# Backward pass of sliding-window attention and a gated unit: another unit order, another filler rule, and a few far units turned by DMA

## The chip, the core and the metric

The kernel runs on one core of one Trainium2 chip. The metric is the device time of one execution in microseconds; a value given for a version is the median of its runs. The profile is one further execution, recorded by the hardware profiler; its times are counted from the first instruction of the span. PE is the matrix engine (TensorE), PEld its weight load, ACT is ScalarE, DVE is VectorE, POOL is GpSimd, SP is the engine that only issues transfers.

## The reference

Input x is 2048 rows of 512 bf16 numbers. Branch A is attention with 32 heads of 16 numbers and a causal window of 256 rows; branch B is a gated unit of width 1376. A sigmoid gate g mixes them. The kernel gives the output and the gradients of all seven inputs that carry one.

```python
qkv = (x @ wqkv) -> q, k, v            # 32 heads of 16
scores = q k^T * 16**-0.5              # kept where 0 <= row - col < 256
a = softmax(scores) v @ wo
gate = x @ W_gate ; up = x @ W_up
b = (relu(gate) * up) @ W_down
out = g * a + (1 - g) * b              # g = sigmoid(sum(x * gate_w))
# then the vector-Jacobian product of out with grad_out, for x, wqkv, wo, W_gate, W_up, W_down, gate_w
```

## The kernel before, in words

The kernel has three stages, written one after the other. The first (up to about 252 us) is the gated unit forward and backward. The second is the attention, forward and backward together. The third (from about 718 us) makes the output and the gradient of x. The change is in the second stage only.

**Units.** The attention goes through four head groups c of eight heads each. In a head group it goes through 16 blocks j of 128 query rows. A block meets up to three key blocks kb: its own (role d, the diagonal), the one before (m, the middle) and the one before that (f, the far one), because the window is two blocks wide. The eight heads are taken in two halves of four. A unit is one (c, j, kb, half): 90 in a head group, 360 in all. `units` (L657 to L673) is the list in order. In a block with all three roles the order is m0 f0 d0 m1 d1 f1 (role and half).

**What a unit does.** The main loop (L886) counts steps n, and each engine gets its instructions in the order in which the loop writes them, so this order is the queue of each engine. Unit n makes its scores on PE at step n (`front`, L683, tile ST), ACT takes the exponential (L693, tile Pu), POOL masks it for the roles d and f (L695, L698). At step n+1 PE makes dP (`front_dp`, L707, tile dPT), at n+2 DVE multiplies them (`gradp`, L712, tile Pd). At step n+4 PE makes the row sums and the forward output (`rowsum`, L721 and L723, eight small matmuls into tile BA). Pu and Pd are also needed turned by 128x128 blocks, for the key side (`flip`): either by one DMA from SP for both halves of a pair (L740, written at n+3), or by eight transposes on PE into a PSUM tile `pt` and one copy out of it by ACT or DVE in turn (L750, L752, written at n+4, behind `rowsum`). In head groups 0 to 2 the roles d and m go by DMA, and f by PE.

**The key side.** Five or more steps after a block's last row sums, `cd_piece` (L532) uses the turned tiles, eight small matmuls for each (query block, key block, half), one or two pieces in a step, first in, first out.

**Fillers.** Beside the units PE has work that can be put anywhere: the projections of the next 512 rows (`project_parts`: Q, dO, rows by DMA, K, V, KV; one list `prq` for each quarter of a head group), and the weight gradient of the head group before (`grad_parts`, 16 pieces in `bgq`; four pieces add up in one PSUM tile `wps`, and the fourth copies it out). `credit` decides when: each step earns something, each filler costs something. `held` is true while a weight gradient has been begun and not finished; L957 then goes on with it, and L960 takes a projection only while `held` is false.

**PSUM.** It has eight banks here: four for ST and dPT (tag M), one for the key side (CD), one for BA, and two of tag TR (L523, `attpr`). The tag TR is used by `pt` of `flip`, by `pp` of the projections (L130), by `ptp` of KV (L173) and, for the weight gradients of head groups 0 and 1, by `wps` (L633); these are made during head groups 1 and 2. A PSUM tile is given up when its last reader has read it.

**Buffers in SBUF.** Pair tiles of role m and d have a ring of three each (L688 to L690, tags PPm and PPd); Pu and Pd of role f have two each.

Of the kernel before, what the change touches and what calls it, by code (L numbers as in the profile page):

```python
# [11 lines left out]
BF = mybir.dt.bfloat16  # L12
# [10 lines left out]
def kernel(  # L23
# [20 lines left out]
    nc = tc.nc  # L44
    P = 128
# [10 lines left out]
    DC = D // P  # L56
# [3 lines left out]
    NTG = S // TGW  # L60
# [43 lines left out]
    NP = P // 32  # L104
# [7 lines left out]
    if True:  # L112
        HH = HG // 2
# [4 lines left out]
        def spread(gi, k):  # L118
            rows = slice(32 * k, 32 * k + 32)
            nc.vector.tensor_copy(zt[gi % ZB][rows, :, k, :, :].rearrange("p w t q -> p w (t q)"),  # L120
                                  proj[groups[gi]]["z"][rows, :, :])
# [76 lines left out]
    with ExitStack() as p1, tc.manual_schedule():  # L198
# [43 lines left out]
        half = TPG // 2  # L242
# [105 lines left out]
        for fc in range(FC):  # L348
            for tg in range(NTG):
                k = Step()  # L350
# [97 lines left out]
        for n in range(N1 + 8):  # L448
# [29 lines left out]
            if at(6):  # L478
                f = weights(at(6))
# [34 lines left out]
    if True:  # L514
# [4 lines left out]
        wk = p3b.enter_context(tc.tile_pool(name="attw", bufs=2))  # L519
# [5 lines left out]
        P2 = {}  # L525
# [87 lines left out]
        def load_gw():  # L613
            nc.sync.dma_start(gw_b[:], gate_w.partition_broadcast(P))

        plan = {2: [load_gw], 5: turns("wqkv", A_wqkv, 0, 4, "p0"), 7: turns("wqkv", A_wqkv, 4, 8, "p1"),
                11: turns("wqkv", A_wqkv, 8, 12, "p2"),
                12: turns("Wg", B_W_gate, 0, 4, "x0") + turns("Wg", B_W_gate, 4, 8, "d0"),
                13: turns("Wg", B_W_gate, 8, 12, "x1") + turns("Wu", B_W_up, 0, 4, "d1") + [lambda: clear("Wg")],
                14: turns("Wu", B_W_up, 4, 8, "x2") + turns("Wu", B_W_up, 8, 12, "d2"),  # L620
                15: loads("Wd", B_W_down, 0, "x3") + [lambda: clear("Wu")] + loads("Wd", B_W_down, 4, "d3") + loads("Wd", B_W_down, 8, "p3") + [load_wo]}
# [35 lines left out]
        units = []  # L657
        for c in range(DC):
            for j in range(NT):
                kbs = [k for k in (j - 1, j, j - 2) if k >= 0]  # L660
                for half in range(2):
                    order = kbs if half or len(kbs) < 3 else [kbs[0], kbs[2], kbs[1]]
                    for ki, kb in enumerate(order):
                        u = Unit()
                        u.c, u.j, u.kb, u.half = c, j, kb, half
                        u.first = ki == 0 and half == 0
                        u.last = ki == len(kbs) - 1 and half == 1
                        u.role = ("d", "m", "f")[j - kb]
                        u.pair = u.role == "d" or (u.role == "m" and (c < DC - 1 or j in (3, 5, 7, 9)))
                        u.own = u.role == "f"  # L670
                        u.dma = u.pair or (u.role == "m" and half == 0 and (c < DC - 1 or j < 10))
                        units.append(u)
        NU = len(units)  # L673

        pairs = {}

        def front(u):
            tg, jl = u.j // TPG, u.j % TPG
            z = zt[(u.c * NTG + tg) % ZB]
            KTt = proj[(u.c, u.kb // TPG)][f"K{u.half}"]  # L680
            ksl = slice((u.kb % TPG) * P, (u.kb % TPG + 1) * P)
            ST = ps.tile([P, HH, P], F32, tag="M", bufs=4, name="ST")
            nc.tensor.matmul(ST[:], lhsT=KTt[:, ksl], rhs=z[:, 0, :, jl, :], start=True, stop=True)  # L683
            if not u.own:
                if u.half == 0:
                    kind = "m" if u.c == DC - 1 and u.j == 12 else u.role
                    tag = f"PP{kind}"
                    pairs[(u.c, u.j, u.kb)] = wk.tile([P, 2, 2, HH, P], BF, tag=tag, bufs=3, name=tag)  # L688
                u.PP = pairs[(u.c, u.j, u.kb)][:, u.half, :, :, :]
                u.Pu, u.Pd = u.PP[:, 0, :, :], u.PP[:, 1, :, :]  # L690
            else:
                u.Pu = wk.tile([P, HH, P], BF, tag="Pu", bufs=2, name="Pu")
            nc.scalar.activation(u.Pu[:], ST[:], ACT.Exp)  # L693
            if u.role == "d":
                nc.gpsimd.affine_select(out=u.Pu[:], in_=u.Pu[:], compare_op=ALU.is_ge, fill=0.0, base=0,  # L695
                                        pattern=[[0, HH], [1, P]], channel_multiplier=-1)
            elif u.role == "f":
                nc.gpsimd.affine_select(out=u.Pu[:], in_=u.Pu[:], compare_op=ALU.is_ge, fill=0.0, base=-1,  # L698
                                        pattern=[[0, HH], [-1, P]], channel_multiplier=1)
# [7 lines left out]
            nc.tensor.matmul(u.dPT[:], lhsT=VTt[:, ksl], rhs=z[:, 1, :, jl, :], start=True, stop=True)  # L707

        def gradp(u):
            if u.own:  # L710
                u.Pd = wk.tile([P, HH, P], BF, tag="Pd", bufs=2, name="Pd")
            nc.vector.tensor_tensor(out=u.Pd[:], in0=u.Pu[:], in1=u.dPT[:], op=ALU.mult)  # L712

        def rowsum(u):
# [17 lines left out]
        def flip(u):  # L732
            key = (u.c, u.j, u.kb, "p2")
            if u.role != "f" and key not in P2 and not (u.pair and u.half == 0):
                P2[key] = wk.tile([P, 2, 2, HH, P], BF, tag=f"P2{u.role}", bufs=3, name=f"p2{u.role}")
            if u.dma:
                if u.pair and u.half == 0:
                    return
                hs = slice(0, 2) if u.pair else slice(u.half, u.half + 1)
                nc.sync.dma_start_transpose(out=P2[key][:, hs, :, :, :].rearrange("p b a h q -> p (b a h) q"),  # L740
                                            in_=pairs[(u.c, u.j, u.kb)][:, hs, :, :, :].rearrange("p b a h q -> p (b a h q)"))
                for b in range(2)[hs]:
                    P2[(u.c, u.j, u.kb, b)] = P2[key][:, b, :, :, :]
                return
            eng = ("act", "dve", "act")[copier["i"] % 3] if u.c == 0 else ("act", "dve")[copier["i"] % 2]
            copier["i"] += 1
            pt = psr.tile([P, 2, HH, P], BF, tag="TR", name="pt")
            for a, src in enumerate((u.Pu, u.Pd)):
                for hh in range(HH):
                    nc.tensor.transpose(pt[:, a, hh, :], src[:, hh, :], ident[:])  # L750
            p2 = P2[key][:, u.half, :, :, :] if u.role == "m" else wk.tile([P, 2, HH, P], BF, tag="P2f", bufs=4, name="p2")[:]
            evac(p2, pt[:], eng)  # L752
            P2[(u.c, u.j, u.kb, u.half)] = p2
# [94 lines left out]
        with tc.manual_schedule():  # L848
            ev = {}
            cdq = []  # L850
            bgq = []
            prq = []
# [3 lines left out]
            n = 0  # L856

            held = False
            fed = 1
            early = []  # L860
            late = []

            def background():
                f, more = bgq.pop(0)
                store = f()
                if store is not None:
                    copies.append(store)
                    if len(copies) > 2 or gi + 2 >= len(groups):
                        ev.setdefault(n + 2, []).append(("dma", flush))
                return more  # L870

            def flush():
                while copies:
                    copies.pop(0)()

            def pieces():
                nonlocal credit
# [8 lines left out]
            while n <= NU + LAG or ev or cdq or bgq:  # L886
                now = ev.pop(n, [])
                u = units[n] if n < NU else None
                if u is not None:
                    gi = u.c * NTG + u.j // TPG  # L890
                    if u.first and u.j == 0:
                        sts[u.c] = st.tile([P, NT, 4, P], BF, tag="rows_st", name="rows_st")
                    if u.first and u.j % TPG == 0:
                        if gi + 1 < len(groups):
                            prq = project_parts(*groups[gi + 1]) if gi else second
# [54 lines left out]
                if n >= NU:  # L950
                    if bgq:
                        held = background()
                    elif n > NU + 1:
                        for _ in range(2):
                            if len(S2["grads"]) > DC:
                                S2["grads"].pop(0)()
                elif held and credit > 0.3:  # L957
                    held = background()
                    credit -= 0.65
                elif prq and not held and ((credit > 0.4 and n > fed + 1) or due - n <= len(prq)):  # L960
                    fed = n
                    credit -= (0.44, 0.86, 0.86, 0.1, 0.86, 0.86)[len(prq) - 1]
                    prq.pop(0)()
                    if len(prq) == 4:
                        for k in range(NP):
                            ev.setdefault(n + 1 + k, []).append(("dve", lambda gi=gi, k=k: spread(gi + 1, k)))
                        ev.setdefault(n + 1, []).append(("dma", flush))
                    if not prq:
                        late += plan.get(gi + 1, [])
                elif bgq and len(prq) <= 2 and credit > 0.3:  # L970
                    held = background()
                    credit -= 0.65
# [164 lines left out]
```

## Time and profile before

| | us |
|---|---|
| median of 2 runs | 910.07 |
| the two runs | 909.61 and 910.52 |
| the profiled execution | 911.05 |
| its span in the profile | 909.4 |
| first scores of head groups 0, 1, 2, 3 | 251.7, 353.6, 469.1, 585.0 |
| last scores (unit 359) | 703.0 |

The four head groups thus last 101.9, 115.5, 115.9 and 118.0 us; the first one has no weight gradients beside it. Read the profile as follows. The busy share of an engine is a union of its instructions, and a matmul is recorded with the time until its result is there (a 128x512 matmul 378 ns), while the next one starts before that (0.215 us after it). So the share of PE says how seldom it is empty, and the start-to-start distance says what a matmul costs the queue.

### The profile page before, as it was taken

How to read it: one execution, taken by the hardware profiler on the slowest of the kernel's cores; microseconds unless marked ns; L12 is line 12 of the kernel's file. 1: busy time of each engine (PE TensorE's matmuls, PEld its weight loads, DVE VectorE, ACT ScalarE, POOL GpSimd, SP SyncE). 2: the span in 40 equal slices, each digit the busy share in tenths (PEclk: the TensorE clock that was granted, in tenths of full speed). 3: DMA queues.
4: the chain of work that ended last, by engine and by line, in shares of the span. 5: the costliest groups of instructions: out<-in, count | busy, mean ns of one | idle time of the engine just before them, and what ended most of it. 6: DMA issues, size and time to landing. Idle time of an engine off the chain costs nothing.

```text
span 909.4 us, 26127 instructions
## 1 busy us (share of the span) xinstructions
PE 895.0 (98%) x10711; PEld 566.7 (62%) x10711; DVE 511.8 (56%) x952; ACT 441.3 (49%) x778; POOL 491.7 (54%) x937
## 2 busy tenths in 40 slices
PE   9999999999989999999999999999999999999998
PEld 5555656655657777667776677766777644444445
DVE  4433334324468887678886788876787222333223
ACT  6422232222278777667776677766788211100001
POOL 4644545545267778767777567875677312222221
PEclk9999999999999999999999999999999999999999
DMA  9998879999799999999999989999999998777731
GB/s 301 203 194 186 197 179 207 211 207 216 180 143 158 180 188 194 184 175 156 177 185 187 180 161 182 187 182 184 184 185 186 235 269 227 186 181 185 182 86 46
DMA packets 505575, 169.06 MB, mean 186 GB/s; under 512 B 433456, under 2 KB 504336, under 8 KB 505456
## 3 DMA queue, kind: packets, MB, share of 16 engines
q1 hardware_dynamic: 484816, 145.51, 86.8%
q10 hardware_dynamic: 19008, 17.31, 7.2%
q0 software_dynamic: 1632, 4.59, 1.4%
q8 instruction: 83, 1.36, 0.6%
q14 instruction: 36, 0.29, 0.1%
HBM read 32.28 MB, written 36.24 MB: 75 GB/s over the span
## 4 chain that ended last, share of the span: by engine, by line
PE 80%; DMA 5%; DVE 4%; POOL 3%; issue 3%; SPq 2%; ACT 2%; ACTq 0%; POOLq 0%; DVEq 0%
PE dxps L1062 8%; PE ST L683 8%; PE dPT L707 7%; PE pt L750 6%; PE wps L412 5%; PE wps L637 5%; PE dxps L1066 4%; PE CD L541 4%; PE bps L1035 4%; PE BA L721 4%; PE pp L133 4%; PE dps L414 3%; PE ups L363 3%; PE gps L363 2%; PE CD L544 2%
## 5 line engine op out<-in xcount | busy, mean ns | idle before, releaser
L683 PE MATMUL ST<-z,K 128*128 128x512 bf16 x360 | 135.8, 378 | 2.6 <-DVE PPm L712 1.2
L707 PE MATMUL dPT<-z,V 128*128 128x512 bf16 x360 | 136.0, 378 | 1.9 <-DVE Pd L712 0.5
L695 POOL TENSOR_SCALAR_AFFINE_SELECT PPd<-PPd 128x512 bf16<-128x512 bf16 x126 | 80.0, 635 | 86.7 <-ACT PPd L693 86.7
L377 POOL TENSOR_TENSOR hT<-rg,upm 128x512 bf16<-128x512 bf16 x44 | 51.8, 1176 | 116.0 <-DVE upm L375 104.3
L412 PE MATMUL wps<-dgu_r,x_r 128*128 128x256 bf16 (+1 forms) x704 | 103.9, 270 | 1.8 <-DVE wst L74 1.8
L712 DVE TENSOR_TENSOR PPd<-PPd,dPT 128x512 bf16<-128x512 bf16 x126 | 85.4, 678 | 18.3 <-PE dPT L707 9.1
L698 POOL TENSOR_SCALAR_AFFINE_SELECT Pu<-Pu 128x512 bf16<-128x512 bf16 x112 | 71.9, 642 | 31.8 <-ACT Pu L693 30.7
L412 PEld LDWEIGHTS <-x_r 128*128 128x128 bf16 x704 | 68.4, 98 | 33.1 <-issue 2.6
L712 DVE TENSOR_TENSOR Pd<-Pu,dPT 128x512 bf16<-128x512 bf16 x112 | 76.3, 681 | 21.5 <-POOL Pu L698 10.6
L693 ACT ACTIVATE PPd<-ST 128x512 bf16<-128x512 f32 x126 | 76.1, 605 | 22.0 <-PE ST L683 19.7
L712 DVE TENSOR_TENSOR PPm<-PPm,dPT 128x512 bf16<-128x512 bf16 x122 | 81.4, 668 | 7.8 <-PE dPT L707 6.1
L693 ACT ACTIVATE Pu<-ST 128x512 bf16<-128x512 f32 x112 | 67.4, 602 | 34.1 <-PE ST L683 33.6
L693 ACT ACTIVATE PPm<-ST 128x512 bf16<-128x512 f32 x122 | 73.7, 604 | 20.2 <-PE ST L683 19.6
L1042 ACT COPY a_sb<-aps 128x512 f32<-128x512 f32 x16 | 9.4, 586 | 151.4 <-issue 137.7
L375 DVE SCALAR_TENSOR_TENSOR upm<-rg,ups 128x512 bf16<-128x512 bf16 x44 | 30.1, 685 | 82.9 <-ACT rg L369 40.3
L369 ACT ACTIVATE rg<-gps 128x512 bf16<-128x512 f32 x44 | 26.3, 598 | 91.8 <-PE gps L363 44.2
L72 ACT COPY p<-pt 128x1024 bf16<-128x1024 bf16 x67 | 68.5, 1022 | 3.8
L414 PE MATMUL dps<-db_r,h_r 128*128 128x512 bf16 x176 | 66.7, 379 | 0.0
L387 POOL TENSOR_TENSOR dgu<-dh_sb,rg 128x512 bf16<-128x512 bf16 x44 | 56.7, 1289 | 5.3 <-ACT dh_sb L383 5.3
L1048 POOL DMA_DIRECT2D out_dram<-o_sb x16 | 8.7, 542 | 88.8 <-DVE o_sb L1046 82.4
L637 PE MATMUL wps<-rows_st,x_r 128*128 128x384 bf16 x256 | 50.3, 325 | 0.0
L133 PE MATMUL pp<-x,p 128*128 128x512 bf16 x192 | 49.0, 378 | 0.0
(193 smaller groups left out, 2357.5 us busy)
## 6 DMA issues: line engine op xcount, KB each, us to landing
dqkvo_d<-rows_st SPq DMA_DIRECT2D x15, 512.0 KB, 4.0
hT_d<-hT ACTq DMA_DIRECT2D x44, 128.0 KB, 2.5
dgT_d<-dgu ACTq DMA_DIRECT2D x44, 128.0 KB, 3.0
duT_d<-dgu ACTq DMA_DIRECT2D x44, 128.0 KB, 2.9
duT_g<-duT_d SPq DMA_DIRECT2D x8, 640.0 KB, 5.2
gt<-hT_d SPq DMA_DIRECT2D x7, 640.0 KB, 5.8
dgT_g<-dgT_d SPq DMA_DIRECT2D x7, 640.0 KB, 5.0
out_dram<-wst SPq DMA_DIRECT2D x20, 128.0 KB, 2.7
```

Of the source, the lines that this page charges most:

```text
L72: nc.scalar.copy(out, in_)
L133: nc.tensor.matmul(pp[:], lhsT=w_p[c][:, cd, which * P:(which + 1) * P], rhs=x_T[tg][:, cd, :], start=(cd == 0), stop=(cd == DC - 1))
L412: nc.tensor.matmul(acc["w"][:, c, 0:2 * nw], lhsT=x_r[:, t, c * P:(c + 1) * P], rhs=k.dgu_r[:, :, i, s0:P], start=(go_ and c % 2 == 0), st ...
L414: nc.tensor.matmul(acc["d"][:], lhsT=k.h_r[:, i, :], rhs=db_r[:, t, :], start=go_, stop=no_)
L637: nc.tensor.matmul(wps[:], lhsT=x_r[:, t, part * P:(part + 1) * P], rhs=sts[c][:, t, 0:3, :], start=first and t == t0, stop=last and t == ...
L683: nc.tensor.matmul(ST[:], lhsT=KTt[:, ksl], rhs=z[:, 0, :, jl, :], start=True, stop=True)
L693: nc.scalar.activation(u.Pu[:], ST[:], ACT.Exp)
L695: nc.gpsimd.affine_select(out=u.Pu[:], in_=u.Pu[:], compare_op=ALU.is_ge, fill=0.0, base=0, pattern=[[0, HH], [1, P]], channel_multiplier=-1)
L698: nc.gpsimd.affine_select(out=u.Pu[:], in_=u.Pu[:], compare_op=ALU.is_ge, fill=0.0, base=-1, pattern=[[0, HH], [-1, P]], channel_multiplier=1)
L707: nc.tensor.matmul(u.dPT[:], lhsT=VTt[:, ksl], rhs=z[:, 1, :, jl, :], start=True, stop=True)
L712: nc.vector.tensor_tensor(out=u.Pd[:], in0=u.Pu[:], in1=u.dPT[:], op=ALU.mult)
L1062: nc.tensor.matmul(to, lhsT=src[:, fc, lsl], rhs=W6[(wt, fc)][:, cols], start=(fc == 0 and wt == "Wg"), stop=False)
```

## The change

The units of a block come in the order m0 m1 f0 d0 d1 f1. In head groups 0 to 2 the half 0 of role f of an odd block (j = 3, 5, ... 15: seven in a head group, 21 in all) is turned by a DMA from SP, written at n+3 like the others, in place of eight PE transposes and a copy. All pair tiles come from one ring of five; a far unit has one tile for Pu and Pd together, in a ring of four. In head groups 0 to 2 the fillers follow a new rule: `todo` counts the fillers that are left in the head group, each step adds `todo` over the steps left to `phase`, and a filler is due when `phase` reaches 1, with a step without a filler between two of them, and rather in a step without PE transposes. If any projection is left it is taken, otherwise a piece of weight gradient. `held` is not asked in this branch. Head group 3 keeps the old rule.

```diff
-                kbs = [k for k in (j - 1, j, j - 2) if k >= 0]
-                for half in range(2):
-                    order = kbs if half or len(kbs) < 3 else [kbs[0], kbs[2], kbs[1]]
-                    for ki, kb in enumerate(order):
...
+                order = [(k, h) for k, h in ((j - 1, 0), (j - 1, 1), (j - 2, 0), (j, 0), (j, 1), (j - 2, 1)) if k >= 0]
+                for kb, half in order:
...
+                    u.dma = u.pair or (u.own and half == 0 and j % 2 == 1 and c < DC - 1) or (u.role == "m" and half == 0 and (c < DC - 1 or j < 10))
...
-                    kind = "m" if u.c == DC - 1 and u.j == 12 else u.role
-                    tag = f"PP{kind}"
-                    pairs[(u.c, u.j, u.kb)] = wk.tile([P, 2, 2, HH, P], BF, tag=tag, bufs=3, name=tag)
+                    pairs[(u.c, u.j, u.kb)] = wk.tile([P, 2, 2, HH, P], BF, tag="PP", bufs=5, name=f"PP{u.role}")
...
-                u.Pu = wk.tile([P, HH, P], BF, tag="Pu", bufs=2, name="Pu")
+                u.PP = wk.tile([P, 2, HH, P], BF, tag="PF", bufs=4, name="PF")
+                u.Pu, u.Pd = u.PP[:, 0, :, :], u.PP[:, 1, :, :]
...
+            if u.dma and u.own:
+                p2 = wk.tile([P, 2, HH, P], BF, tag="P2f", bufs=4, name="p2f")
+                nc.sync.dma_start_transpose(out=p2[:].rearrange("p a h q -> p (a h) q"),
+                                            in_=u.PP[:].rearrange("p a h q -> p (a h q)"))
+                P2[(u.c, u.j, u.kb, u.half)] = p2[:]
+                return
...
+            def project():
+                nonlocal fed, late, todo
+                fed = n
+                todo -= len(prq) != 4
+                prq.pop(0)()
...
+                elif u.c < DC - 1:
+                    if u.first and u.j == 0:
+                        todo = 5 * NTG - (2 if u.c == 0 else 0) + (16 if u.c else 0)
+                    phase = min(1.6, phase + todo / max(4, (u.c + 1) * (NU // DC) - n - 2))
+                    turn = len(prq) == 4
+                    if prq and (turn and n > fed + 1 or due - n <= len(prq)):
+                        project()
+                        phase -= not turn
+                    elif phase >= 1 and (w is None or w.dma or phase > 1.5) and n > fed + 1 and (prq and not turn or bgq):
+                        phase -= 1
+                        if prq:
+                            project()
+                        else:
+                            fed = n
+                            todo -= 1
+                            held = background()
                 elif held and credit > 0.3:
```

## The prediction

> **What bounds the kernel now.** I read the page first, for the engine that carries the end.
>
> ```profile
> PE 895.0 (98%) x10711; PEld 566.7 (62%) x10711; DVE 511.8 (56%) x952; ACT 441.3 (49%) x778; POOL 491.7 (54%) x937
> ...
> PEclk9999999999999999999999999999999999999999
> ...
> PE 80%; DMA 5%; DVE 4%; POOL 3%; issue 3%; SPq 2%; ACT 2%; ACTq 0%; POOLq 0%; DVEq 0%
> ```
>
> PE is almost never empty, its clock is full, and the chain that ended last is PE's. Then the windows of the four head groups and of the stretch behind them (length, then busy time of PE, PEld, DVE, ACT, POOL, granted clock, DMA share):
>
> ```profile
> 251.70:353.60 101.90, 99.39 (x1765) 69.58 (x1764) 81.53 (x155) 81.05 (x145) 77.22 (x180) 1.00 1.02 171
> 353.60:469.10 115.50, 115.03 (x2011) 81.00 (x2007) 89.29 (x168) 83.65 (x150) 84.83 (x197) 1.00 1.09 176
> 469.10:585.00 115.90, 115.05 (x2011) 80.86 (x2008) 90.44 (x168) 83.14 (x149) 84.78 (x197) 1.00 1.09 180
> 585.00:703.00 118.00, 116.36 (x2087) 84.59 (x2084) 88.85 (x162) 86.95 (x153) 83.94 (x195) 1.00 1.11 184
> 703.00:718.00 15.00, 14.41 (x250) 10.79 (x248) 3.37 (x6) 4.35 (x9) 7.38 (x19) 1.00 1.07 235
> ```
>
> PE is empty for 2.5, 0.5, 0.9, 1.6 and 0.6 us of these: 6.1 us is all that smoother feeding can win. DVE, ACT and POOL have 20 to 30% to spare, and the DMA share stands at about one (packets overlap, so that this is not yet full). So the time of this stage is PE's queue: what leaves it is won whole, and any new wait in it is lost whole. For what a turned unit costs there, and for how soon a PSUM bank comes free, I read a timeline with a projection (dO) and a PE flip behind it (start, duration; a matmul's duration includes its way to PSUM, so distances between starts are what counts):
>
> ```profile
> 385.96 1.02 PE L136 MATMUL pp<-d,p 128*128 128x512 bf16 x4
> 386.82 0.38 PE L683 MATMUL ST<-z,K 128*128 128x512 bf16 x1
> ...
> 387.02 0.69 DVE L74 CAST zT<-pp 128x512 bf16<-128x512 f32 x1 [0.18 <-PE pp L136]
> ...
> 387.24 0.38 PE L750 MATMUL pt<-ident,Pu 128*128 128x128 bf16 x4
> 387.46 0.39 PE L750 MATMUL pt<-ident,Pd 128*128 128x128 bf16 x4
> 387.69 0.38 PE L707 MATMUL dPT<-z,V 128*128 128x512 bf16 x1
> ...
> 387.94 1.01 ACT L72 COPY p<-pt 128x1024 bf16<-128x1024 bf16 x1
> 388.11 0.38 PE L683 MATMUL ST<-z,K 128*128 128x512 bf16 x1
> ```
>
> The flip starts at 387.24, while DVE empties the bank of dO until 387.71. That costs nothing here: there are two TR banks.
>
> **Transposes that leave PE.** A flip takes 387.69 - 387.24 = 0.45 us of the queue; over all flips eight starts of 55 ns, 0.44 us. 21 units x 0.44 = **9.2 us** less, 3.1 in each of head groups 0 to 2. Their copies (1.02 us on ACT, 0.68 on DVE) lie beside PE and are worth nothing by themselves. ST, dP, row sums and key pieces keep their number and place; head group 3 keeps all its flips.
>
> **Fillers, and the TR banks.** The work of the fillers is the same. Their order is not, and I followed both rules step by step. Before, a weight gradient once begun is finished before a projection starts, in four or five steps. In the new branch a projection goes first whenever one is left. In head group 1 (units 90 to 179) the first piece of a weight gradient comes at step 106 and opens a TR bank; then a new quarter begins and Q 108, dO 110, K 114, V 116 and KV 118 go ahead, and the gradient ends at 125. The second runs from 127 to 146 around the projection of 132 to 142, the third from 149 to 168 around 156 to 166; the fourth (170 to 178) meets none. Head group 2 repeats it 90 steps later. So in six of the eight quarters a whole projection and the flips beside it share **one** TR bank: each user waits on PE for the copy of the one before. Queued behind that wait is all of PE. The trace of before has no such case, so I work it out from the rows:
> - dO, flip in the next step: in the timeline the flip would wait from 387.24 to 387.71, 0.47 us.
> - Flip of f0 and K in the same step: only dP and one key piece (0.42 us) lie between, K would start at 388.11, the ACT copy ends at 388.95: 0.84 us. A DVE copy ended 0.95 to 2.4 us after the last transpose in this stage (the late ones behind the spread copies of L120, 0.56 us each, that follow dO): 0.5 to 1.9 us; I take 1.3.
> - V, flip in the next step: the ACT cast ended 1.00 us after V's last start, the flip comes 0.63 us after it: 0.37 us.
> - Flip, KV in the next step: 1.1 us of PE work between, copy on ACT 1.32 us after: 0.2 us; on DVE behind the masks of K and V (L169) 1.75 us: 0.65 us.
>
> Flips go to ACT and DVE in turn. By the count, f0 before K falls to ACT in head group 1 and to DVE in head group 2. Head group 1: 0.47 + 0.84 + 0.37 + 0.65 = 2.33, three times 7.0. Head group 2: 0.47 + 1.3 + 0.37 + 0.2 = 2.34, three times 7.0. Sum **14.0 us**. Bounds: 0 if something else gives these banks back, and with every copy late (0.5 + 1.9 + 0.6 + 0.9) x 6 = 23. I take 14.0 because each term has a row of this stage.
>
> **The unit order.** Both m come first, then four masked units in a row. POOL has 0.64 us of mask for each of these (L695, L698), and 1.04 us of small work in the sixth step, 0.83 in each of the two after. Before, one of these two fell on a masked unit (1.47 us in a step of 1.28); now both fall on m. In head group 3 three flips come in a row from block 10 on; with two banks and copies in turn that is 2.5 us for each bank, so free. Together between -3 us (half of the empty 6.1) and +2; I take -1.
>
> **Transfers and rings.** SP issues in order. A pair's DMA holds SP for 2.7 us (median, 1.77 at least), and a 128x1024 one, the size of the new ones (rows, L181), 1.26. In head group 1 SP's transfers take 95 of 115.5 us, so 7 x 1.26 = 8.8 us more makes 104 of some 113. The new DMA stands behind that of its block's m pair and ahead of that of its d pair. It is written at step n+3 and needed nine steps on, 11.5 us: 2.7 + 1.26 + 3.3 (median landing of rows) = 7.3, hidden. With the ring of five a pair tile is wanted again 11 steps after its DMA is written (before 12 or 13), 8 to 10 at the start of a head group. In block 5 of head group 2 the product ended at 512.92, the DMA began at 516.58, behind that of m, and landed at 520.93: 8.0 us or 6.3 steps. Now m and d are three steps apart and the queue between them is shorter. So 0, with up to +5 where a head group starts.
>
> **Sum**, against the profiled execution: 911.05 - 9.2 + 14.0 - 1 = 914.9. The median of the runs is 0.98 lower, so **914**.
>
> **Rivals.** *The gain stays* (0.25). PE's waits for a bank are as rare as before, because the copies come sooner in a queue that waits, or a bank is returned in another way. For it: PE waited for a flip's copy only 0.2 us in the whole trace (step 321). Against it: no flip and no projection there ran beside an open weight gradient with under two steps between them. Time: 911.05 - 9.2 - 2 (a third of the empty time) = 899.9, so 899.
>
> *SP becomes the bound* (0.12, the other side). Place: SP's queue in head groups 0 to 2. If pairs take 3.2 us, as several in head group 2 did, 31 of them make 99, the rest of SP's work there 12.6, the new ones 10 with some wait: 122 us in a head group of 113 to 117. It decides from the point where SP's sum passes PE's; then exponentials wait for a pair tile and PE behind them. Price: 122 - 116 = 6 for each of three, and the bank waits hide beneath it: 911 + 18 = 929; half of it gives 920. Against it: SP often sits idle (409.4 to 413.2 us, say), so the 2.7 us are partly waiting.
> The Trainium skill (VectorE: DVE Perf Modes, sections "The three transpose paths" and "Rules for kernel authors") would not move these units at all: it gives 390 ns for a 128x128 block on TensorE and 1309 ns by DMA, and advises TensorE where PSUM will do. Taken at its word, eight blocks would occupy the transfers 10.5 us (an estimate from that page) and this rival would be certain; the trace disagrees, 2.7 us for 16 blocks.
>
> *The fillers are not made even* (0.08). `phase` stands at its cap of 1.6 when a quarter opens, so the five projections still come every second step or so, and their waits and the saved transposes cancel: 908 to 912, say 910.
>
> **Chances.** The forecast, 905 to 921, has 0.55; gain stays 0.25 (896 to 905), SP 0.12 (920 to 932), nothing moves 0.08. For 8 in 10 the range takes the forecast, the third rival and most of the first, and the mild half of the SP case: 899 to 921. 2% (18 us) is about what a measurement of this kernel can tell from no change: below 892 all the transposes and all the empty time together (15.3 us) don't reach, 0.01; above 928 only the heavy SP case, 0.05; within 0.94.
>
> **What would show it.** Right: no PE flips of f0 in odd blocks (L750 loses 168 transposes); the first head group shorter by about 3 us; head groups 1 and 2 longer by 1 to 5 us, with PE's idle time there ahead of `pt`, `pp` and `ptp`, released by copies of TR tiles. Wrong: all three groups shorter by 3 us (no bank waits), or waits of ACT for PP tiles and of PE for turned tiles (SP). A head group 3 that moved by over 2 us would contradict what I said of the order.

## The result, and the profile after

| | us |
|---|---|
| after, median of 2 runs | 923.19 (921.38 and 925.01) |
| before, median of 2 runs | 910.07 |
| ratio after : before | 1.014, 95% interval 1.012 to 1.016 |
| the profiled execution of after, its span | 925.01, 923.3 |

The changed kernel is slower by 13 us: the direction that was forecast, with a size 9 us over the forecast and 2 us above its range. From the page of after, the busy time of the engines, PE's clock and the chain that ended last:

```profile
PE 894.0 (97%) x10543; PEld 560.5 (61%) x10543; DVE 501.8 (54%) x944; ACT 429.4 (47%) x765; POOL 494.7 (54%) x937
...
PEclk9999999999999999999999999999999999999999
...
PE 30%; DVE 0%; issue 0%; ACT 0%
```

PE's busy share fell only from 98 to 97%, but its empty time (span less busy time) doubled, from 14.4 to 29.3 us. Busy time itself fell by 1.0 us, not by the 9.2 us of the 168 transposes that left it, in part because a matmul at half clock counts as busy for longer. The chain could be followed back over 30% of the span only, so its shares say nothing of the stage here (order_rings below, with hardly a wait of PE in head groups 1 and 2, has a chain of 28%). The clock looks full, but one digit stands for 23 us. The windows of after show the rest: first the four head groups and the 15 us behind them, then three short stretches (columns as before: length, busy time of PE, PEld, DVE, ACT, POOL, granted clock, DMA share):

```profile
250.20:354.60 104.40, 98.72 (x1707) 67.07 (x1706) 78.63 (x153) 77.67 (x140) 78.07 (x179) 0.98 1.11 177
354.60:473.40 118.80, 113.44 (x1956) 78.42 (x1953) 86.52 (x164) 79.47 (x145) 84.94 (x196) 1.00 1.15 192
473.40:599.20 125.80, 115.39 (x1953) 79.03 (x1950) 87.65 (x165) 78.95 (x145) 85.46 (x197) 0.97 1.10 183
599.20:717.60 118.40, 116.72 (x2091) 85.00 (x2087) 88.69 (x163) 87.04 (x153) 85.29 (x196) 1.00 1.05 185
717.60:732.60 15.00, 14.54 (x256) 10.93 (x254) 3.41 (x7) 4.17 (x8) 7.21 (x19) 1.00 1.05 207
...
351.20:354.60 3.40, 3.40 (x43) 2.01 (x41) 2.02 (x4) 1.97 (x4) 1.86 (x4) 0.51 1.12 116
487.70:491.10 3.40, 3.27 (x31) 1.61 (x31) 0.20 (x1) 1.48 (x5) 1.96 (x4) 0.50 1.10 226
576.40:579.80 3.40, 3.40 (x46) 1.84 (x44) 1.81 (x4) 1.68 (x3) 0.34 (x2) 0.50 0.93 174
```

Against 101.9, 115.5, 115.9 and 118.0 us before, the head groups changed by +2.5, +3.3, +9.9 and about 0; what lies ahead of and behind them became 2 us shorter together. The last three lines are new: three stretches of 3.4 us in which PE got half its clock, one in head group 0 and two in head group 2.

Next, PE's own waits in after, by tile (the tile and line that waited, what released it; us in total, times, longest):

```profile
PE pp L133 <- DVE p L74: 5.8, 3, 1.9
PE CD L541 <- DMA p2f<-PF: 3.1, 2, 1.7
PE dPT L704 <- ACT PPd L690: 2.8, 3, 1.9
PE pt L751 <- DVE zT L74: 2.3, 6, 0.4
PE pp L133 <- ACT p L72: 2.1, 3, 0.7
PE pt L751 <- ACT VT L72: 1.7, 6, 0.3
```

Four of the six are waits of a projection or a flip for the copy that empties a TR bank, the forecast's mechanism. The second is PE waiting for a far unit turned by the new DMA. The third holds a wait of PE behind ACT, which itself waited for a pair tile. Here are such waits in the timeline of after (start, duration; the bracket is the idle time before the instruction and what ended it):

```profile
320.70 0.19 PE L541 MATMUL CD<-rq,p2f 128*128 128x32 bf16 x1 [1.37 <-DMA p2f<-PF]
...
380.68 1.02 PE L136 MATMUL pp<-d,p 128*128 128x512 bf16 x4
...
381.74 0.69 DVE L74 CAST zT<-pp 128x512 bf16<-128x512 f32 x1 [0.85 <-PE pp L136]
...
382.48 0.61 PE L751 MATMUL pt<-ident,PF 128*128 128x128 bf16 x8 [0.38 <-DVE zT L74]
...
487.18 0.60 ACT L690 ACTIVATE PPd<-ST 128x512 bf16<-128x512 f32 x1 [1.71 <-DMA p2d<-PPd]
...
506.38 0.61 PE L751 MATMUL pt<-ident,PF 128*128 128x128 bf16 x8
506.58 0.77 DVE L120 COPY z<-zT 32x1024 bf16<-32x1024 bf16 x1
507.39 0.69 DVE L707 TENSOR_TENSOR PPd<-PPd,dPT 128x512 bf16<-128x512 bf16 x1
508.11 0.44 DVE L120 COPY z<-zT 32x1024 bf16<-32x1024 bf16 x1
508.57 0.69 DVE L74 COPY p<-pt 128x1024 bf16<-128x1024 bf16 x1
509.32 1.02 PE L133 MATMUL pp<-x,p 128*128 128x512 bf16 x4 [1.93 <-DVE p L74]
```

At 382.48 the flip starts only when DVE has emptied the bank of dO (before, the same flip started beside the copy). At 506.38 the flip of f0 is done on PE by 507.0, but its copy is fourth in DVE's queue, behind two spread copies and a product; K, which needs the bank, starts at 509.32. Counted from start to start (the distance between two starts, less what the first matmul costs the queue: 215 ns with 512 columns, 55 with 128, 25 with 16 to 33), 24 TR waits cost 6.5 us in head group 1 and 10.0 us in head group 2.

The last view is SP's queue in head group 0 of after:

```profile
303.81 3.50 SPq L741 DMA_TRANSPOSE p2m<-PPm  x1
307.36 0.57 SPq L564 DMA_DIRECT2D dqkvo_d<-rows_st  x1
308.05 3.64 SPq L741 DMA_TRANSPOSE p2d<-PPd  x1
311.79 1.25 SPq L181 DMA_TRANSPOSE rows<-zT  x1
313.13 2.88 SPq L741 DMA_TRANSPOSE p2m<-PPm  x1
316.11 1.46 SPq L733 DMA_TRANSPOSE p2f<-PF  x1
317.67 3.13 SPq L741 DMA_TRANSPOSE p2d<-PPd  x1
```

Each transfer starts about 0.1 us after the end of the one before; nothing is idle. Adding up SP's transfers and its gaps of over 0.5 us in head groups 0, 1 and 2:

| | SP transfers, us | SP idle, us |
|---|---|---|
| before | 83.9 / 96.2 / 98.5 | 13.6 / 15.7 / 13.0 |
| after | 99.3 / 112.0 / 113.4 | 1.9 / 0 / 8.2 |

From the product of a far unit to the start of its transfer, the seven new transfers of head group 0 waited 2.6, 2.2, 4.7, 6.7, 7.0, 8.4 and 5.6 us: the queue falls behind as the group goes on.

### The profile page after: what moved, and what is told of

Read it like the earlier page. It is cut to its first block, busy times and chain, and to the rows that moved or that the text cites. A ratio compares the mean times of both kernels' runs of the same rounds, so it can differ in the third digit from the quotient of the medians.

```text
span 923.3 us, 25855 instructions
## 1 busy us (share of the span) xinstructions
PE 894.0 (97%) x10543; PEld 560.5 (61%) x10543; DVE 501.8 (54%) x944; ACT 429.4 (47%) x765; POOL 494.7 (54%) x937
## 5 line engine op out<-in xcount | busy, mean ns | idle before, releaser
L695 POOL TENSOR_SCALAR_AFFINE_SELECT PF<-PF 128x512 bf16<-128x512 bf16 x112 | 71.7, 641 | 50.8 <-ACT PF L690 49.0
L690 ACT ACTIVATE PPm<-ST 128x512 bf16<-128x512 f32 x120 | 71.8, 600 | 38.3 <-PE ST L681 36.0
L707 DVE TENSOR_TENSOR PPm<-PPm,dPT 128x512 bf16<-128x512 bf16 x120 | 80.7, 681 | 11.6 <-PE dPT L704 10.5
L707 DVE TENSOR_TENSOR PF<-PF,dPT 128x512 bf16<-128x512 bf16 x112 | 76.2, 680 | 17.5 <-PE dPT L704 11.2
L690 ACT ACTIVATE PF<-ST 128x512 bf16<-128x512 f32 x112 | 67.3, 601 | 32.9 <-PE ST L681 27.4
L751 PE MATMUL pt<-ident,PF 128*128 128x128 bf16 x728 | 55.5, 219 | 4.0 <-DVE zT L74 2.3
L72 ACT COPY p<-pt 128x1024 bf16<-128x1024 bf16 x49 | 50.1, 1022 | 2.9 <-PE pt L751 0.9
```

## The experiments

The theories to tell apart: **bank waits** (a weight gradient that stays open in one of two TR banks while a whole projection goes ahead makes PE wait) and **SP's queue** (the 21 added transfers fill it, and turned tiles and pair tiles come late). A ratio is against the kernel before, run on the same chip (medians 909.7 to 910.2), with its 95% interval. The medians of two experiments can come from two chips.

### finish_first: after, with a weight gradient finished before a projection starts

```diff
-                    if prq and (turn and n > fed + 1 or due - n <= len(prq)):
+                    if prq and (not held and turn and n > fed + 1 or due - n <= len(prq)):
...
-                        if prq:
+                        if prq and not held:
```

> The changed kernel, but a projection waits until a weight gradient that was begun is finished. Bank theory: the PE waits ahead of pt, pp and ptp in head groups 1 and 2 (6.5 and 10.0 us in the changed kernel's trace) go, and with them most stretches of half clock (three of 3.4 us, worth about 1.5 us each): 923.2 - 16.5 - 3 = 904, between 901 and 908; head groups 1 and 2 each last 112 to 114 us, head group 0 stays at 104. SP theory (SP's queue is what holds head groups 0 to 2 back, and the bank waits only lie on top of it): with PE quicker the waits for turned tiles and pair tiles grow, head groups 1 and 2 stay at 116 to 118 us, time 911 to 916.

Measured: 913.74, ratio 1.005 [1.003, 1.006]; head groups 102.4, 119.9, 115.5, 118.6. The TR waits are gone and 9.4 us with them, so the bank mechanism is real. But that is less than the 16.5 us of those waits, and the kernel stays 4 us above the one before although 9.2 us of transposes have left PE: the time is that of the SP theory. The two largest waits of PE that are left in it:

```profile
PE CD L541 <- DMA p2f<-PF: 4.0, 3, 2.5
PE BA L716 <- ACT BAs L722: 2.3, 2, 2.1
```

and its timeline in head group 1, ACT's lines and SP's queue:

```profile
403.22 3.28 SPq L741 DMA_TRANSPOSE p2d<-PPd  x1
406.56 1.30 SPq L581 DMA_TRANSPOSE p<-in_A_wqkv_dram  x1
407.96 3.02 SPq L741 DMA_TRANSPOSE p2m<-PPm  x1
411.09 3.12 SPq L741 DMA_TRANSPOSE p2d<-PPd  x1
414.30 2.22 SPq L741 DMA_TRANSPOSE p2m<-PPm  x1
...
409.18 1.08 ACT L690 ACTIVATE PPm<-ST 128x512 bf16<-128x512 f32 x2 [2.49 <-DMA p2d<-PPd]
...
414.45 0.60 ACT L690 ACTIVATE PPd<-ST 128x512 bf16<-128x512 f32 x1 [3.03 <-DMA p2m<-PPm]
```

Read the two together: the exponential at 409.18 needs the pair tile that the transfer of 403.22 gives back (it landed at 409.1), and the one at 414.45 that of 407.96, which had stood behind it in a queue without a gap. ACT waited for 2.5 and 3.0 us, and PE behind the second of these (the 2.1 us ahead of BA). Three more waits of ACT, of 2.0 to 3.3 us, are for a far tile, and each ended with the same landing as a wait of PE for `p2f`. SP is idle for 1.9, 0 and 0 us in this kernel. This is SP's queue as the limit, free of bank waits.

### far_on_pe: after, with every far unit turned by PE

```diff
-                    u.dma = u.pair or (u.own and half == 0 and j % 2 == 1 and c < DC - 1) or (u.role == "m" and half == 0 and (c < DC - 1 or j < 10))
+                    u.dma = u.pair or (u.role == "m" and half == 0 and (c < DC - 1 or j < 10))
```

> The changed kernel, but all far units are turned on PE, none by DMA. Bank theory: 168 transposes come back (+9.2 us), the three waits for late transfers go (1.5 + 1.9 us ahead of CD in head group 0, 2.1 us of ACT for a pair tile in head group 2), the bank waits stay at 16 to 18 us: 924 to 930, head group 0 near 102 us. SP theory: the time drops below 917, since SP has 30 us less to issue.

Measured: 923.77, ratio 1.016 [1.015, 1.018]; head groups 101.6, 122.2, 122.3, 118.6. No added transfer, SP idle for 10.4, 24.7 and 28.4 us, and still 14 us lost, nearly all in head groups 1 and 2, the two with weight gradients beside them. SP's queue alone is refuted. Start to start, the TR waits are about 13.8 us here, 2 us under the 16 to 18 that were expected.

### fill_only: the kernel before, with the new filler rule and nothing else

```diff
+            phase = 0.0
+            todo = 0
...
+            def project():
...
+                elif u.c < DC - 1:
...
```

> The kernel before with the new filler rule alone; old unit order, old rings, all far units on PE. Bank theory: bank waits of 12 to 18 us in head groups 1 and 2 and nothing else, perhaps one stretch of half clock: 921 to 929. SP theory, or a loss that comes from order and rings: 908 to 913, as before.

Measured: 923.35, ratio 1.015 [1.014, 1.017]; head groups 103.5, 121.8, 121.8, 118.1. From its waits of PE:

```profile
PE pt L750 <- DVE KV L192: 3.0, 6, 0.5
...
PE pt L750 <- DVE zT L74: 2.3, 6, 0.4
```

Six times each, once for every quarter that meets an open weight gradient. The filler rule alone costs 13.7 us, in the old order and with the old rings. Of these 11.6 are TR waits, counted from start to start; head group 0, which has none, is longer by 1.6 as well, with three waits of PE ahead of ST for a product of DVE.

### old_fillers and order_rings: after with the old filler rule, far units by DMA or all on PE

```diff
-                elif u.c < DC - 1:
+                elif False:
```

(and in order_rings the edit of far_on_pe as well).

> The changed kernel with the filler rule of before in all head groups; unit order, DMA turns and rings as changed. Bank theory: no projection runs beside an open weight gradient, so as finish_first, 901 to 908 us. If even spacing has a worth of its own, it is some us above finish_first. SP theory: 911 to 916.

> The changed kernel with the old filler rule and all far units on PE, so that only the unit order and the rings of the change are left. Two-cause theory (bank waits from the filler rule, and SP's queue full through the 21 added transfers): neither cause is in it, so 908 to 912, as before (909.7), with SP idle for over 10 us in each of head groups 1 and 2. Rival (order or rings hold the transfers back by themselves): 913 or more, with waits of ACT for pair tiles.

Measured: old_fillers 917.85, ratio 1.009 [1.008, 1.011], above what either theory gave; order_rings 911.43, ratio 1.002 [1.001, 1.003], as the two-cause theory had it. So unit order and rings alone lose 1.2 us, and the added transfers lose 6.4 us on top in place of winning 9.2. Old_fillers also has two half-clock stretches, at 442.1 and 588.9 us, right behind waits of PE of 3.1 and 2.5 us.

### ff_far_pe and ff_few: finish_first with none, or 9, of the 21 units turned by DMA

ff_far_pe makes the edit of far_on_pe in finish_first; ff_few this one:

```diff
-                    u.dma = u.pair or (u.own and half == 0 and j % 2 == 1 and c < DC - 1) or (u.role == "m" and half == 0 and (c < DC - 1 or j < 10))
+                    u.dma = u.pair or (u.own and half == 0 and j in (5, 9, 13) and c < DC - 1) or (u.role == "m" and half == 0 and (c < DC - 1 or j < 10))
```

> As finish_first, but all far units on PE: order, rings and even spacing without the bank waits and without the added transfers. Two-cause theory: 908 to 912. If even spacing has a worth of its own, the difference from order_rings shows it; I expect under 1.5 us.

> As finish_first, but by DMA only the far units of half 0 of blocks 5, 9 and 13 (9 in place of 21). Two-cause theory: SP had 13 to 16 us idle in each head group before, the three transfers take 4 of them, so nothing waits; 9 x 0.44 = 4.0 us of transposes are won: 904 to 907. If any added transfer costs as much as it saves, whatever SP's idle time: 908 to 912.

Measured: ff_far_pe 908.88, ratio 0.9984 [0.9975, 0.9992]; ff_few 907.98, ratio 0.9978 [0.9969, 0.9986]. Both are faster than the kernel before, by 1.5 and 2 us. The even spacing is worth 2.5 us here (order_rings to ff_far_pe), more than the 1.5 expected. The windows of ff_few, head groups 0 to 2:

```profile
249.70:350.70 101.00, 98.17 (x1718) 68.25 (x1730) 79.01 (x154) 79.06 (x142) 77.46 (x179) 1.00 1.11 181
350.70:465.80 115.10, 113.25 (x1977) 79.47 (x1986) 89.18 (x168) 80.91 (x147) 86.29 (x198) 1.00 1.16 192
465.80:580.10 114.30, 112.81 (x1969) 79.38 (x1980) 89.07 (x167) 81.22 (x147) 85.24 (x197) 1.00 1.13 184
```

The clock is full in all three. But nine units off PE are 9 x 0.44 = 4.0 us by the prediction's price, and the time fell by 0.9 us, hardly clear of the spread of the runs, to the edge of both expectations. SP is idle for only 2.4 to 3.7 us in a head group here, yet in its trace no wait of PE or ACT of over 0.15 us in head groups 0 to 2 was ended by a turned tile or a pair tile. So late transfers don't explain the missing 3 us. In the profiled executions these three groups together are 1.4 us shorter than in ff_far_pe, with some new small waits for products of DVE (0.4 to 0.5 us), and head group 3, which the edit leaves alone, is 0.9 us longer; the cause stays open.

The six kernels with the new order form a table (us, medians):

| filler rule | all far units on PE | 21 by DMA | the DMAs add |
|---|---|---|---|
| old | order_rings 911.43 | old_fillers 917.85 | +6.4 |
| new, gradient finished first | ff_far_pe 908.88 | finish_first 913.74 | +4.9 |
| new | far_on_pe 923.77 | after 923.19 | -0.6 |

The medians of the first two rows come from two chips; by the ratios to before the differences are +6.8 and +5.6. In the third row the difference is within the spread of the runs. Only where PE already loses some 14 us to the banks do the transfers break even; that the longer head groups 1 and 2 then give SP some of the time it lacks is my reading, not a run's.

### fill_finish: fill_only with the gradient finished first

```diff
-                    if prq and (turn and n > fed + 1 or due - n <= len(prq)):
+                    if prq and (not held and turn and n > fed + 1 or due - n <= len(prq)):
...
-                        if prq:
+                        if prq and not held:
```

> The kernel before with the new filler rule that finishes a begun weight gradient first; old unit order, old rings, all far units on PE. order_rings was 1.2 us above before, ff_far_pe 2.5 below order_rings. If order and even spacing add up: 910.2 - 2.5 = 907.7, between 906.5 and 909. If even spacing wins only with the new order: 909.5 to 911.

Measured: 913.02, ratio 1.003 [1.002, 1.005], above both. Without bank waits the even spacing won 2.5 us in the new unit order (order_rings to ff_far_pe) and lost 3 us in the old one, where PE waits ahead of ST for a product that DVE makes late (2.8 us in six waits). The order, or the rings that came with it, and the spacing belong together; no run has the new order with the old rings.

### wps_in_m: after, with the weight gradients in the other banks

```diff
-                    own, tag, bufs = (ps, "M", 4) if c + 2 >= DC else (psr, "TR", 2)
+                    own, tag, bufs = ps, "M", 4
```

> The changed kernel with the weight gradients of all head groups in the M banks, as those of head group 2 are already, so that both TR banks stay free for flips and projections while the order of the fillers stays as changed. Bank theory: the waits ahead of pt, pp and ptp in head groups 1 and 2 fall from 16.5 us to under 2, some new ones ahead of ST and dPT come (three M banks); the transfers stay, so about finish_first: 912 to 918. If the order of the fillers itself is the cause, whatever bank they use: 921 or more.

Measured: 926.46, ratio 1.018 [1.016, 1.020]; head groups 102.5, 124.4, 122.3, 118.3. Three of its largest waits of PE:

```profile
PE dPT L704 <- DVE PPm L707: 3.2, 7, 0.9
PE CD L541 <- DMA p2f<-PF: 2.6, 2, 1.5
PE ST L681 <- ACT PPm L690: 2.1, 6, 0.4
```

The waits for TR banks are gone, and in the same steps scores and dP now wait for one of three M banks instead of four. So it isn't the ring that matters: a weight gradient stays open for 19 steps, and whichever ring lends the bank pays.

### ff_split and ff_pool: what fills SP's queue

ff_split makes two transfers of each pair, with the same bytes; ff_pool issues the row spills and the weight-gradient stores from POOL in place of SP. Both start from finish_first.

```diff
+                for b in range(2)[hs]:
+                    one = slice(b, b + 1)
+                    nc.sync.dma_start_transpose(out=P2[key][:, one, :, :, :].rearrange("p b a h q -> p (b a h) q"),
+                                                in_=pairs[(u.c, u.j, u.kb)][:, one, :, :, :].rearrange("p b a h q -> p (b a h q)"))
```

```diff
-            eng = nc.gpsimd if (c == DC - 1 and t0 + TPG == NT) else nc.sync
+            eng = nc.gpsimd
...
-                return lambda: nc.sync.dma_start(to, ws[:])
+                return lambda: (nc.sync if tail else nc.gpsimd).dma_start(to, ws[:])
```

> As finish_first, but each pair is turned by two DMAs of one half each, issued one behind the other: the same bytes, 93 transfers more on SP. If SP's issuing has a fixed part for each DMA that is the limit (a 128x1024 transpose took SP 1.23 us at least, a pair 1.77 at least, so 0.69 us more for two halves): some 20 us more SP work in a head group, 925 us or more. If SP only waits for the transfer engines, whose work is unchanged: 911 to 917 (finish_first 913.7).

> As finish_first, but the spills of rows_st and the stores of the weight gradients of head groups 0 to 2 are issued from POOL, which takes 2 to 6 us off SP in a head group and leaves the bytes as they are. If SP's own issuing is the limit: 904 to 910 (finish_first had 913.7), late turned tiles become rare. If the transfer engines behind SP are the limit, so that SP only waits for them: 912 to 915, and SP's transposes become longer by what the others gave up.

Measured: ff_split 935.01, ratio 1.027 [1.026, 1.028]; ff_pool 922.43, ratio 1.014 [1.012, 1.015]. Two lines of SP's queue in ff_split:

```profile
418.28 2.96 SPq L743 DMA_TRANSPOSE p2d<-PPd  x2
421.35 2.67 SPq L743 DMA_TRANSPOSE p2m<-PPm  x2
```

Two halves together hold the queue about as long as one whole (a half 1.45 us on average, a whole 2.78 in finish_first), and with the gap of 0.10 us between them a split costs some 0.23 us more, 7 us for the 31 pairs of a head group. So in a full queue the price of a transposing transfer goes mainly by its bytes, with some 0.2 us for each transfer. The time came out where the expectation put a fixed part of 0.69 us, but the fixed part is a third of that; in a queue without idle time it was enough to add 21 us, five half-clock stretches included. ff_pool missed both expectations: the stores left SP, but POOL then made its own tile `rq` late (PE waited up to 1.6 us for it, 6.5 us in seven waits), and pairs held SP for 2.9 to 3.0 us, one of them for 7.3, beside a wait of PE of 4.1 us, the longest. But its profiled execution took 929.5 us, 7 more than the median, so these waits are more than the usual ones. Whether SP itself or the transfer engines behind it set the time per byte stays open.

## Why the prediction was right or wrong

**Transposes that leave PE, -9.2: right.** Count times start-to-start distance gives PE's own work as 3.1 us less in each of head groups 0, 1 and 2, and the same in 3.

**Fillers and the TR banks, +14.0: right in place and cause, 2.5 short.** far_on_pe and fill_only, which have these waits without the added transfers, lost 14.1 and 13.7 us. In after they come to 6.5 and 10.0 where 7.0 and 7.0 was forecast. Two of the terms held: dO to flip 0.52 (forecast 0.47) and V to flip 0.43 (0.37). Flip to KV, 0.35 and 0.31, was forecast as 0.65 and 0.2, too much in one group and too little in the other. The term that was mis-sized is f0 to K: on ACT it was 0.84 as forecast, on DVE 2.07 in place of 1.3, three times. There the copy stood behind two spread copies and a product. The trace of before had such a row (head group 0):

```profile
277.01 0.42 DVE L120 COPY z<-zT 32x1024 bf16<-32x1024 bf16 x1
...
277.58 0.64 DVE L712 TENSOR_TENSOR PPm<-PPm,dPT 128x512 bf16<-128x512 bf16 x1
278.25 0.70 DVE L120 COPY z<-zT 32x1024 bf16<-32x1024 bf16 x1
278.99 0.69 DVE L74 COPY p<-pt 128x1024 bf16<-128x1024 bf16 x1
```

This copy ended 2.38 us after the last transpose had started, the upper end of the prediction's 0.95 to 2.4. I took a value in the middle instead of the row that fitted.

**Unit order, -1: wrong in sign, small.** order_rings lost 1.2 us with it and the rings, which no run separates. They pay only with the even spacing, in kernels where neither bank waits nor added transfers are in the way (ff_far_pe, 908.88, against fill_finish, 913.02).

**Transfers and rings, 0: this is the step that failed.** I took the latency of one transfer (7.3 us of 11.5) and asked whether it was hidden; the question was whether a queue that already had 95 of 115.5 us of work could take more. The added transfers held SP for 1.7, 1.4 and 1.6 us on average in head groups 0, 1 and 2 (single ones 1.24 to 2.38), not 1.26; pairs became 0.1 us longer, and each transfer is followed by a gap of some 0.1 us that my sum left out (112.0 us of transfers fill 118.8 with no gap over 0.5). SP's sum in head group 1 rose by 15.8 us, not 8.8, and its idle time went from 15.7 us to none. The wait for SP's turn, put at 2.7 us, grew to 8.4. In the profile of after this shows as 1.53 and 1.89 us of PE waiting for `p2f` in head group 0, and 2.09 us of PE behind ACT's wait for a pair tile in head group 2, 5.5 us together, where the prediction put nothing. The table of six kernels gives the real price of the step: where no bank waits mask it, 21 transfers cost about 14 to 16 us (9.2 + 4.9, 9.2 + 6.4), as much as the banks do. A full queue doesn't cost by itself, though: in head group 3 of before SP's transfers take 110.4 of 118.1 us, with 1.9 us idle (only 25 of its 66 transfers turn units), and no wait of PE or ACT there was ended by a turned tile or a pair tile.

**Half-clock stretches: not foreseen.** Three times 3.4 us at half clock cost 1.4, 1.3 and 1.2 us, counted from start to start, 3.9 together. Each follows a wait of PE of about 1.9 to 2.1 us: one for `p2f`, one behind the pair tile, one for the bank of K. So they are a second price of the same waits. The other execution of after, 3.6 us shorter, had a mean granted clock of 0.998 instead of 0.994; one stretch is worth about 0.002, so it probably had one instead of three.

**The sum.** Head group 0 was forecast at -3.1 and came out at +2.5: 3.4 of `p2f` waits and 1.4 of half clock account for 4.8 of the 5.6 us between. Head group 1 was forecast at about +3.9 and came out at +3.3. Head group 2 was forecast at +3.9 and came out at +9.9: 3.0 more bank waits, 2.1 behind the pair tile and 2.5 of half clock, 7.6 us where 6.0 are needed; the other small waits of that group were 1.6 us less than before. The profiled execution was also 1.8 us above the median of after.

**The rivals.** *The gain stays* and *the fillers are not made even* fell: the bank waits are there. *SP becomes the bound*, with 0.12, named the right place and the right sign, the exponential that waits for a pair tile; pairs did not need the 3.2 us of its condition, 2.7 to 2.8 sufficed. "SP often sits idle" spoke against it only until the added work was set against that idle time. And I had taken it as an alternative to the forecast; both happened, for the most part in different head groups, and their sum was left out of the likeliest range. That the time lies in this rival's range (920 to 932) is luck: by its account the bank waits hide beneath SP's, and here they are the larger part of the loss. As for the rule weighed there (the Trainium skill, VectorE: DVE Perf Modes, sections "The three transpose paths" and "Rules for kernel authors"), its advice to turn on TensorE where PSUM will do would have been right for 12 of the 21 units (finish_first against ff_few, 5.8 us) and about even for the other nine (ff_few against ff_far_pe, 0.9 us the other way). Its 1309 ns for a block does not carry over to eight in one transfer: the trace of after gives 1.4 to 1.7 us for all eight.

**What would show it.** Of the signs of being right, L751 lost its 168 transposes, head group 1 is longer by 3.3, and PE waits ahead of `pt`, `pp` and `ptp`; head group 0 shorter by 3 did not come, and head group 2 overshot. The signs named for SP, waits of ACT for PP tiles and of PE for turned tiles, are in the profile as well. Head group 3 moved by 0.3 us, within the 2 us allowed.

## What to carry to other kernels

Before moving work to a queue that issues in order, set the whole added time, gaps included, against that queue's idle time in the stage; a latency that fits says nothing about a queue that is full. Count for how many steps an accumulator holds its PSUM bank and what else uses the ring meanwhile: 19 steps in one of two banks cost 14 us here, and another ring didn't help; finishing it first did. When the forecast and a rival sit in different places of the stage, give a chance to both at once.

## What the runs showed of the hardware

**Half clock after a window that is half empty.** All stretches at half clock in the attention stage last 3.41 us (one in ff_pool 6.83), and within a kernel they lie on one grid: they start at 351.15, 487.69 and 576.43 us in after, 40.0 and 26.0 times 3.413 us apart; in old_fillers 43.0 times, in ff_split 13.0, 16.0, 16.0 and 22.0 times. So I cut the stage of these kernels into windows of that grid and added up the time in which PE had no matmul:

| kernel | empty in the windows just ahead of a stretch, us | largest in any other window, us |
|---|---|---|
| after | 1.93, 1.78, 1.72 | 1.60 |
| finish_first | 2.11 | 1.59 |
| old_fillers | 2.98, 2.35 | 0.94 |
| ff_split | 2.84, 2.07, 1.77, 1.76, 1.58 | 1.53 |
| ff_pool | 3.10, 1.83, 1.74 | 1.56 |

Half a window is 1.71 us. The two columns part at about 1.6 us, with one overlap (1.58 was followed by half clock in ff_split, 1.60 was not in after), so what is empty within one window seems to decide: in after the wait ahead of the projection at 509.32 is as long as those with half clock behind them, but a border of the grid (508.2) cuts it in two, and nothing followed. In finish_first a wait of 2.49 us was cut into 1.59 and 0.90 in the same way. One case does not fit: the stretch of 6.83 us in ff_pool went on after a window with 1.02 us empty, one that had itself run at half clock. In the kernels without a stretch (before, far_on_pe, fill_only, fill_finish, order_rings, ff_far_pe, ff_few, wps_in_m) no single wait of PE in this stage was above 1.6 us. The Trainium skill (TensorE: Matmul & The Clock Gate, section "Part 1: The HAM clock gate") has a free-running window of 3413 ns, which these starts bear out, and lets the clock fall after an idle window; here a window about half empty was enough.

**Half clock doubles the wide matmuls, not the narrow ones.** From the first stretch of after:

```profile
352.04 0.63 PE L681 MATMUL ST<-z,K 128*128 128x512 bf16 x1
352.46 0.63 PE L704 MATMUL dPT<-z,V 128*128 128x512 bf16 x1
```

They start 427 ns apart instead of 215 (those with 128 columns 107 instead of 55), while those with 16 to 33 columns still follow each other after 25 to 30 ns. So a stretch of 3.41 us cost 1.2 to 1.4 us in after, less than the 1.7 that half the clock would take.

**A transposing transfer between SBUF tiles** held SP, on average by kernel, for 2.5 to 3.0 us for 128x2048 and 1.4 to 1.6 us for 128x1024 elements (the shortest 1.62 and 1.24), in a queue where the next transfer started about 0.1 us after the last had ended. The averages go mainly by bytes; the shortest ones do not.
